# SBUF start addresses of matmul operands in a fused attention and MLP kernel: tiles moved to one byte address modulo 256

## The chip, the cores and the metric

The kernel runs on one core of one Trainium2 chip. The metric is device time in microseconds of one execution. The profile is one execution on the chip, taken by the hardware profiler. Engines are named PE (TensorE matmul), PEld (TensorE weight load), DVE (VectorE), ACT (ScalarE), POOL (GpSimd) and SP (the queue that issues most DMAs); L12 is line 12 of the kernel.

## The reference

One input x of 2048 tokens with 448 features goes through two branches, mixed by a gate per token. `_gelu` is the tanh approximation, `_layernorm` subtracts the mean and divides by the root of variance plus 1e-5.

```
def _A_ref(x, wq, wk, wv, wo):                      # 16 heads of 28, one shared key and value head
    q = (x @ wq).reshape(B, S, H, Dh).transpose(0, 2, 1, 3)
    k = x @ wk; v = x @ wv
    p = _softmax(einsum("bhqd,bkd->bhqk", q, k) * Dh ** -0.5)
    o = einsum("bhqk,bkd->bhqd", p, v)
    return o.transpose(0, 2, 1, 3).reshape(B, S, H * Dh) @ wo

def _B_ref(x, w1, w2, w3, w4):
    h = _gelu(_layernorm(x) @ w1)                   # 448 x 448
    hs = concat(four quarters of h, shifted by +1, -1, +2, -2 tokens) @ w2
    x1 = x + hs
    return x1 + _gelu(_layernorm(x1) @ w3) @ w4     # w3 448 x 1792, w4 1792 x 448

g = sigmoid((x * gate_w).sum(-1))
out = g * _A_ref(x) + (1 - g) * _B_ref(x)
```

## The kernel before

Tokens are taken in four blocks b of 512. The work goes through three stages, each with its own pool of SBUF tiles.

Stage 1 (pools s1 and s1b) projects queries, keys, values and gate (`stage_q`, with the halves wqh and wql of the weights), then does the first two MLP products (`stage_w1`, `stage_w2`). To keep precision, a matrix is split into a high part rounded to the format that TensorE multiplies in one pass, and a low part, the rest. `proj` (L134 to L140) then makes a product out of 11 matmuls: three chunks c of 128 features with high x high, low x high and high x low, and two for the last 64 features, whose high and low parts of x share one tile. In `proj`, wh and wl are the weights that are loaded into the array (LDWEIGHTS), ah and al the values that are moved through it. `stage_w1` does four column groups m of 112 columns for each block, 16 groups in all. The profile names its output h, and that of the query projection q.

Stage 2 (pool s2, and s2a on the right side of the memory) does w3 and w4. For each block b it runs a loop over f, 14 chunks of 128 hidden features. Turn f makes g, the product with w3 (`w3_part`: `proj` with ah3 and al3 moved and a column group of w3h and w3l as weights, 11 matmuls of 512 columns), takes its Gelu into gh (high) and gl (low), and then does the product of chunk f - 2 with w4 into the four accumulators acc (`w4_part`, L692 to L694: 12 matmuls of 448 columns, in which the slices of gh and gl of 128 tokens are the weights and w4h and w4l are moved). The last chunk of the last block is left to the attention stage (gf_late, w4_late). The matrices w3 and w4 lie in seven pieces of two chunks. Pieces 0 to 2 (f = 0 to 5) come from s2a, pieces 3 to 6 (f = 6 to 13) from s2, whose tiles follow those of the pool `keep` low in the memory.

Stage 3 (pool s3) is attention. There are 16 units u (block b, group g of four heads) with 16 key tiles kt of 128 keys each. A cycle handles two key tiles. `scores` (L205) does three rounds for a tile (qh with kh, ql with kh, qh with kl), each of four matmuls at once, one head in each 32 rows of the array; a slice of kh or kl of 128 keys is the weight, the queries qh and ql of 512 tokens are moved. ACT takes exponentials (L871) into p, partly after a DVE copy (L928). `values` (L882) multiplies p, moved, with vext, the values of one key tile, as weights, in single precision, and `wo_products` (L830) the result with wo. Unit 0 uses the queries qh0 and ql0, which come from another pool than qh and ql of the later units.

Instructions of all engines are written out in the order in which they run; no scheduler moves them. A pool gives a tile its byte address in each partition by the order and size of allocation, in whole steps of 32 bytes. The start addresses modulo 256 that this gives for the operands of the matmuls (a chunk or slice adds a multiple of 256, except where several are listed):

| product | moved | weights |
|---|---|---|
| q (L136 to L140) | x, 224 | wqh, wql, 224 |
| h (w1), m = 0, 1, 2, 3 | x, 224 | w1h, w1l, 224, 160, 96, 32 |
| g (w3), f = 0 to 5 | ah3, al3, 160 | w3h, w3l, 160 |
| g (w3), f = 6 to 13 | ah3, al3, 160 | w3h, w3l, 224 |
| acc (w4), f = 0 to 5 | w4h, w4l, 160 | gh, gl, 224 |
| acc (w4), f = 6 to 13 | w4h, w4l, 224 | gh, gl, 224 |
| scores, unit 0 | qh0, ql0, 32 | kh, 32; kl, 128 |
| scores, later units | qh, ql, 160 | kh, 32; kl, 128 |
| values | p, 160 | vext, 128 and 0 by turns |
| wo | wof, 224 and 96 | on, 160 and 32 by turns |
| w4 of the last chunk | w4_late, 32 and 160 | gf_late, 32 and 160 by turns |

Of the kernel before, what the change touches and what calls it, by code (L numbers as in the profile page):

```python
# [9 lines left out]
F32 = mybir.dt.float32  # L10
F32R = mybir.dt.float32r
# [6 lines left out]
P = 128  # L18
S = 2048
D = 448  # L20
# [3 lines left out]
C = D // 4  # L24
NB = S // 512
NT = S // P
# [11 lines left out]
def f32(ap):  # L38
    return ap.bitcast(F32)
# [3 lines left out]
def gated_mix_kernel(  # L43
# [14 lines left out]
    keep = ctx.enter_context(tc.tile_pool(name="keep", bufs=1))  # L58
# [8 lines left out]
    ident = keep.tile([P, P], F32, name="ident")  # L67
    make_identity(nc, ident)
    x1 = keep.tile([P, NT, D], F32, name="x1")
    kl = keep.tile([P, S], F32R, name="kl")  # L70
    vext = keep.tile([P, NT, 32], F32, name="vext")
    gz = keep.tile([P, NT], F32, name="gz")
    gg = keep.tile([P, NT], F32, name="gg")
    gi = keep.tile([P, NT], F32, name="gi")
    first = keep.tile([P, 4], F32, name="first")
    epst = keep.tile([P, 4], F32, name="epst")
    powt = keep.tile([P, 4], F32, name="powt")
    invE = keep.tile([P, NT], F32, name="invE")
    qd = dram.tile([NG, P, S], F32, name="qd")
    nc.gpsimd.memset(epst, EPS)  # L80
# [29 lines left out]
    def split_w_high(raw, wh, wl):  # L110
        nc.scalar.copy(wh[:, 0:3, :], raw[:, 0:3, :])
        nc.gpsimd.memset(f32(wh)[64:128, 3, :], 0.0)
        nc.scalar.copy(wh[0:64, 3, :], raw[0:64, 3, :])
        nc.scalar.copy(wl[64:128, 3, :], raw[64:128, 3, :])

    def split_w_low(raw, wh, wl):
        for c in range(3):
            nc.vector.tensor_tensor(wl[:, c, :], raw[:, c, :], f32(wh)[:, c, :], ALU.subtract)
        nc.vector.tensor_tensor(wl[0:64, 3, :], raw[0:64, 3, :], f32(wh)[0:64, 3, :], ALU.subtract)
# [14 lines left out]
    def proj(ps, wh, wl, ah, al):  # L134
        for c in range(3):
            nc.tensor.matmul(ps, wh[:, c, :], ah[:, c, :], start=(c == 0), stop=False)  # L136
            nc.tensor.matmul(ps, wh[:, c, :], al[:, c, :], start=False, stop=False)  # L137
            nc.tensor.matmul(ps, wl[:, c, :], ah[:, c, :], start=False, stop=False)  # L138
        nc.tensor.matmul(ps, wh[:, 3, :], ah[:, 3, :], start=False, stop=False)  # L139
        nc.tensor.matmul(ps, wl[:, 3, :], ah[:, 3, :], start=False, stop=True)  # L140
# [119 lines left out]
    with tc.tile_pool(name="s1b", bufs=1) as s1b, \  # L260
            tc.tile_pool(name="ps1", bufs=1, space=PSUM) as ps1:
        s1_stack = ExitStack()
        s1 = s1_stack.enter_context(tc.tile_pool(name="s1", bufs=1))
        turn = [0]

        def mm1(name):
            k = turn[0] % 4
            turn[0] += 1
            return mm_tile(name) if k < 2 else ps1.tile([P, 512], F32, tag="tp", bufs=2, name=name)
# [22 lines left out]
            nc.scalar.dma_start(wqraw[:, c, :], wq[:, c, :])  # L292
            nc.sync.dma_start(xraw[0][:, c, :], xT[:, c, 0:512])
        nc.scalar.activation(first, powt, AF.Gelu_apprx_tanh)
        w1h = s1.tile([P, 4, D], F32R, name="w1h")
        w1l = s1.tile([P, 4, D], F32R, name="w1l")
        w2h = s1b.tile([P, 4, D], F32R, name="w2h")
        w2l = s1b.tile([P, 4, D], F32R, name="w2l")
        hh, hl, acts = {}, {}, {}
# [31 lines left out]
        def stage_q(u, tile_of=mm1):  # L331
            b, g = divmod(u, NG)
            ps = tile_of(f"q_{u}")
            w = slice(g * P, (g + 1) * P)
            proj(ps, wqh[:, :, w], wql[:, :, w], *xact[b])
            q_out(u, ps)
# [91 lines left out]
        def spare_h(b):  # L428
            low = f32(hl[b])
            nc.sync.dma_start(shifted(hh[b], 0, 2), low[0:32, 0, 1:513])  # L430
            nc.sync.dma_start(shifted(hh[b], 2, 2), low[32:64, 0, 1:513])
            nc.sync.dma_start(shifted(hl[b], 1, 2), low[64:96, 0, 1:513])
            nc.sync.dma_start(shifted(hl[b], 3, 1), low[96:112, 0, 1:513])
# [4 lines left out]
        def stage_w1(b, between=None):  # L438
            hh[b] = s1b.tile([P, 4, 516], F32R, tag="hh", bufs=2, name=f"hh_{b}")
            hl[b] = s1b.tile([P, 4, 516], F32R, tag="hl", bufs=2, name=f"hl_{b}")  # L440
            for tt in (hh, hl):
                if b == 0:
                    nc.gpsimd.memset(f32(tt[b])[0:C, :, 0:2], 0.0)
                else:
                    nc.gpsimd.tensor_copy(tt[b][0:C, :, 0:2], f32(tt[b - 1])[0:C, :, 512:514])
            for m in range(4):
                ps = mm1(f"h_{b}_{m}")
                w = slice(m * C, (m + 1) * C)
                proj(ps[0:C, :], w1h[:, :, w], w1l[:, :, w], *xact[b])
                if between:  # L450
                    between(m)
                hf = s1.tile([P, 512], F32, tag="hf", bufs=3, name=f"hf_{b}_{m}")
                nc.vector.tensor_mul(hf[0:C, :], ps[0:C, :], rb_of[b][0:C, :])
                nc.scalar.activation(hh[b][0:C, m, 2:514], hf[0:C, :], AF.Gelu_apprx_tanh)
                nc.scalar.activation(hf[0:C, :], hf[0:C, :], AF.Gelu_apprx_tanh)
                nc.gpsimd.tensor_tensor(hl[b][0:C, m, 2:514], hf[0:C, :], f32(hh[b])[0:C, m, 2:514],
                                        ALU.subtract)
            if b in (0, 2):
                spare_h(b)
            for tt in (hh, hl):  # L460
                if b:
                    nc.gpsimd.tensor_copy(tt[b - 1][0:C, :, 514:516], f32(tt[b])[0:C, :, 2:4])
                if b == NB - 1:
                    nc.gpsimd.memset(f32(tt[b])[0:C, :, 514:516], 0.0)
# [16 lines left out]
        w1raw = f32(s1b.tile([P, 4, 516], F32R, tag="hl", bufs=2, name="w1raw"))[:, :, 0:D]  # L481
# [28 lines left out]
        centre_w1()  # L510
        stage_q(7)
        stage_q(8)
        split_w_high(w1raw, w1h, w1l)
        split_w_low(w1raw, w1h, w1l)
        for t in range(4):
            ln1_tile(1, t)
        stage_q(9)
# [9 lines left out]
        def first_between(m):  # L527
# [3 lines left out]
            if m == 2:  # L531
                ln1_send(1)
                ln1_read(1)
                spare_w2()

        stage_w1(0, first_between)

        def second(m):
# [4 lines left out]
            else:  # L543
                ln1_tile(2, 2 * m // 3)
                ln1_tile(2, 2 * m // 3 + 1)

        stage_w1(1, second)
        stage_kv(0)
        stage_kv(1)
# [11 lines left out]
        ln1_tile(3, 3)  # L561
        mv0, rs0 = stats_tiles(s1, "m")
        stage_w1(2, lambda t: stats_tile(s1, 0, t, mv0))
        stats_end(mv0, rs0)
        ln1_send(3)
# [93 lines left out]

    with tc.tile_pool(name="s2", bufs=1, reuse_waits="tile") as s2, \  # L660
            tc.tile_pool(name="ps2", bufs=1, space=PSUM, reuse_waits="tile") as ps2:
        def weigh_x1(n0, n1):
            for n in range(n0, n1):
                nc.gpsimd.tensor_scalar(x1[:, n, :], x1[:, n, :], gi[:, n:n + 1], None, op0=ALU.mult)
# [31 lines left out]
        for b in range(NB):  # L696
            acc = [ps2.tile([P, 512], F32, tag="acc", bufs=4, name=f"acc_{b}_{t}") for t in range(4)]
            gs = {}
            for f in range(NF):
# [22 lines left out]
                if b == NB - 1 and f == 4:  # L722
                    weigh_x1(0, 4 * b)
# [31 lines left out]
    with tc.tile_pool(name="s3", bufs=1, reuse_waits="tile") as s3, \  # L755
# [92 lines left out]
            if g == NG - 1 and u < NU - 1 and cols.stop == D:  # L848
                nc.sync.dma_start(out[0, n * P:(n + 1) * P, :], ot_of[n])

        pick = s3.tile([P, 4], F32, name="pick")
        nc.gpsimd.memset(pick, 0.0)
        for j in range(4):
            nc.gpsimd.memset(pick[32 * j:32 * j + 1, j:j + 1], 1.0)
# [1 line left out]
        nc.gpsimd.memset(ones, 1.0)  # L856

        weigh_x1(NT - 4, NT)

        def w4_products(t, ps, cols):  # L860
# [51 lines left out]
        for c in range(NC):  # L912
            u, i = divmod(c, NT // 2)
            k = 2 * c
            s0, s1, s2, s3_ = singles if c % 2 == 0 else singles[2:] + singles[:2]
# [19 lines left out]
            if i == 3 and norms:  # L935
                w = norms[0][0]
# [107 lines left out]
        with tc.If(again > 0, label="redo"):  # L1044
            for b in range(NB):
                for g in range(NG):
# [7 lines left out]
                    for kt in range(NT):  # L1054
                        ps = [bank(f"s2_{u}_{kt}_{j}") for j in range(4)]
                        scores(u, kt, ps)
                        p = s3.tile([P, 4, 512], F32, tag="p", bufs=PB, name=f"p2_{u}_{kt}")
# [65 lines left out]
```

## Time and profile before

| | |
|---|---|
| median of 3 runs | 924.17 us (922.94 to 924.70) |
| the profiled execution | 923.3 us |
| its span, first to last instruction | 921.4 us |
| mean granted TensorE clock | 0.999 |
| stage 1 and 2, up to the first score of unit 0 | 0 to about 401 us, of it w3 and w4 from 125 us |
| attention | about 401 us to the end |

The page of the profile first gives the busy time of each engine with its share of the span, then the chain of work that ended last. In rows of groups, the numbers behind the bar are busy time, the mean duration of one instruction in ns and the idle time just before. A matmul's duration runs on while the next one has started, so that several lie over each other; how far apart two matmuls start is read from the starts, or from a window that holds a known number of them. In rows of windows stand the stretch in us from the span's start, its length, the busy time of PE with the number of instructions that touch the window, the granted clock, the DMA share and GB/s. In rows of the timeline stand start (us), length (us), engine, line, operation and, at the end, how many equal instructions are merged into the row.

### The profile page before, as it was taken

The page shows a single profiled execution, that of the slowest core. Times are in us where ns is not written, and L with a number is a line of the kernel's source. Part 1 is how long each engine was busy: PE and PEld are TensorE (multiplying, and loading weights), DVE is VectorE, ACT ScalarE, POOL GpSimd, SP SyncE. Part 2 cuts the span into 40 slices and gives each one's busy share as a digit, 9 for nine tenths or more (in the row PEclk, how much of TensorE's full clock was granted, in tenths as well). Part 3 has the DMA queues.
Part 4 walks back from the last instruction along what each step waited for, and adds up shares of the span by engine and source line. Part 5 has one row for each costly group of instructions (what it writes and reads, how often), then busy time and mean ns, then how long its engine had stood idle before and what let it go on. Part 6 is the DMA issues. An engine that isn't in the chain of part 4 may idle for free.

```text
span 921.4 us, 24273 instructions
## 1 busy us (share of the span) xinstructions
PE 908.7 (99%) x10360; PEld 625.4 (68%) x10360; DVE 519.2 (56%) x962; ACT 635.1 (69%) x1002; POOL 79.1 (9%) x116
## 2 busy tenths in 40 slices
PE   9999999999999999999999999999999999999997
PEld 6788888888888888865555555555555555555554
DVE  4664264631431431156766767677667667676664
ACT  5442445322222232169999999999999999999994
POOL 3243420200000520020000000000000000000000
PEclk9999999999999999999999999999999999999999
DMA  8832643120110110010000001000001000010001
GB/s 305 292 88 59 172 149 109 40 66 1 41 47 1 40 46 1 1 51 24 17 22 22 16 17 53 24 25 15 25 33 37 22 20 19 15 54 14 15 14 43
DMA packets 40583, 47.32 MB, mean 51 GB/s; under 512 B 10136, under 2 KB 28632, under 8 KB 40472
## 3 DMA queue, kind: packets, MB, share of 16 engines
q1 hardware_dynamic: 37304, 40.30, 14.6%
q10 hardware_dynamic: 3168, 5.44, 1.6%
q8 instruction: 82, 1.34, 0.6%
q14 instruction: 29, 0.24, 0.1%
HBM read 32.56 MB, written 11.67 MB: 48 GB/s over the span
## 4 chain that ended last, share of the span: by engine, by line
PE 94%; ACT 4%; issue 1%; DMA 1%; DVE 0%; ACTq 0%; DVEq 0%
PE bank L882 26%; PE bank L205 17%; PE bank L830 6%; PE acc L694 5%; PE acc L692 5%; PE acc L693 5%; PE g L137 4%; PE g L138 4%; PE g L136 4%; ACT p L871 4%; PE pair L205 2%; PE hs L471 1%; PE hs L472 1%; PE g L140 1%; PE g L139 1%; PE h L136 1%
## 5 line engine op out<-in xcount | busy, mean ns | idle before, releaser
L871 ACT ACTIVATE p<-bank 128x512 f32<-128x512 f32 x512 | 265.6, 613 | 10.5 <-POOL ones L856 4.3
L882 PE MATMUL bank<-p,vext 128*32 128x256 f32 x4064 | 247.6, 382 | 6.5 <-ACT p L871 1.7
L882 PEld LDWEIGHTS bank<-p,vext 128*32 128x32 f32 x4064 | 117.6, 109 | 124.6 <-ACT p L871 61.8
L928 DVE COPY p<-pair 128x1024 f32<-128x1024 f32 x127 | 155.6, 1225 | 59.0 <-PE pair L205 46.8
L682 ACT ACTIVATE gh<-g 128x512 fp32r<-128x512 f32 x55 | 32.9, 598 | 186.4 <-PE g L140 186.4
L804 DVE TENSOR_TENSOR o<-o,bank 128x256 f32<-128x256 f32 x222 | 93.6, 422 | 85.4 <-PE bank L882 74.1
L871 ACT ACTIVATE p<-p 128x1024 f32<-128x1024 f32 x127 | 140.0, 1103 | 0.0
L871 ACT ACTIVATE p<-pair 128x1024 f32<-128x1024 f32 x129 | 137.7, 1067 | 0.0
L684 DVE TENSOR_TENSOR gl<-gf,gh 128x512 fp32r<-128x512 f32 x55 | 38.2, 694 | 169.0 <-ACT gf L683 169.0
L205 PE MATMUL bank<-qh,kh 32*128 32x512 f32 x512 | 114.8, 442 | 0.0
L205 PE MATMUL pair<-qh,kh 32*128 32x512 f32 x512 | 114.3, 441 | 0.3 <-DVE x L749 0.3
L205 PE MATMUL bank<-qh,kl 32*128 32x512 f32 x512 | 101.9, 390 | 0.0
L205 PE MATMUL pair<-qh,kl 32*128 32x512 f32 x512 | 101.6, 390 | 0.0
L205 PE MATMUL bank<-ql,kh 32*128 32x512 f32 x512 | 101.2, 388 | 0.0
L205 PE MATMUL pair<-ql,kh 32*128 32x512 f32 x512 | 100.7, 388 | 0.0
L205 PEld LDWEIGHTS bank<-qh,kh 32*128 32x128 f32 x512 | 48.2, 181 | 61.4 <-issue 37.3
L694 PE MATMUL acc<-w4h,gl 128*128 128x448 f32 x220 | 80.4, 366 | 0.0
L692 PE MATMUL acc<-w4h,gh 128*128 128x448 f32 x220 | 80.3, 365 | 0.0
L693 PE MATMUL acc<-w4l,gh 128*128 128x448 f32 x220 | 80.1, 364 | 0.0
L830 PE MATMUL bank<-wof,on 128*32 128x224 f32 (+1 forms) x984 | 69.5, 357 | 0.3 <-DVE o L804 0.2
L137 PE MATMUL g<-al,w3h 128*128 128x512 f32 x168 | 65.9, 393 | 0.0
L138 PE MATMUL g<-ah,w3l 128*128 128x512 f32 x168 | 65.9, 392 | 0.0
(206 smaller groups left out, 1394.6 us busy)
## 6 DMA issues: line engine op xcount, KB each, us to landing
qd<-qf ACTq DMA_DIRECT2D x15, 256.0 KB
rb<-rd SPq DMA_DIRECT2D x15, 256.0 KB
x<-in_x_dram SPq DMA_DIRECT2D x4, 896.0 KB
xd<-xt SPq DMA_DIRECT2D x16, 224.0 KB
w34raw<-in_w_dram SPq DMA_DIRECT2D x7, 512.0 KB
qr<-qd SPq DMA_DIRECT2D x64, 56.0 KB
w34raw<-in_w_dram SPq DMA_DIRECT2D x7, 448.0 KB
out_dram<-ot SPq DMA_DIRECT2D x14, 224.0 KB
```

The costliest lines, as they stand in the source:

```text
L136: nc.tensor.matmul(ps, wh[:, c, :], ah[:, c, :], start=(c == 0), stop=False)
L137: nc.tensor.matmul(ps, wh[:, c, :], al[:, c, :], start=False, stop=False)
L138: nc.tensor.matmul(ps, wl[:, c, :], ah[:, c, :], start=False, stop=False)
L205: nc.tensor.matmul(ps[j], k[h, keys], q[h, :], start=(r == 0), stop=(r == 2), tile_position=(32 * j, 0))
L692: nc.tensor.matmul(ps, gh[:, tok], w4h[i][:, k, :], start=(f == 0), stop=False)
L693: nc.tensor.matmul(ps, gh[:, tok], w4l[i][:, k, :], start=False, stop=False)
L694: nc.tensor.matmul(ps, gl[:, tok], w4h[i][:, k, :], start=False, stop=(f == stop))
L804: nc.vector.tensor_add(o, o, pv)
L830: nc.tensor.matmul(ps[32 * i:32 * i + 32, :], a[:, c:c + 32], w, start=start, stop=stop, tile_position=(0, 32 * i))
L871: nc.scalar.activation(p[:, heads], p[:, heads] if source is None else source, AF.Exp, scale=SCALE)
L882: nc.tensor.matmul(pv[32 * j:32 * j + 32, :], vext[:, kt, :], p_of[k][:, j, qs], start=(k == ks[0]), stop=(k == ks[-1]), tile_position=(0, ...
L928: nc.vector.tensor_copy(pa[:, both], pairs[0])
```

## The change

Tiles get other start addresses. In the pool `keep`, which lies lowest, three tiles of 16 bytes a partition and gz are allocated ahead of kl and vext, which moves kl from 128 to 32 modulo 256, and vext with it. In stage 1, w1h and w1l get 512 columns for 448: each group of 112 columns now starts at a multiple of 128 columns, so all four start at 224, and the split of w1 writes rows of 112 columns with gaps of 16 between. In stage 2 an unused tile of 192 bytes (gap2) is put ahead of the tiles of s2, which moves gh, gl, gf and pieces 3 to 6 of w3 and w4 from 224 to 160. The size of `keep` as a whole stays the same. In stage 3, pick is allocated with 36 columns and used with 4, so that the tiles behind it move on by 128 bytes: qh, ql, p, o and on go from 160 to 32. Tiles on the right side of the memory stay where they were, kh among them.

Afterwards the table reads: h 224 and 224 in all four groups; g 160 and 160 in all 14 turns; acc 160 and 160 in all turns; scores 32 for queries, kh and kl; values 32 for p, and 32 and 160 by turns for vext; wo 224 and 96 with 32 and 160; q and w4_late as before.

Every engine issues the same operations in the same order. Besides the addresses, the access patterns of the split of w1 change (three ACT copies, four DVE subtractions, a POOL memset), and some waits for DMAs that follow from which tile used an address before: ACT waits for the loads of vT at the first gf of stage 2 instead of at the first piece 3 of w3, and POOL waits for other loads of kl in the split of the keys.

```
     x1 = keep.tile([P, NT, D], F32, name="x1")
-    kl = keep.tile([P, S], F32R, name="kl")
-    vext = keep.tile([P, NT, 32], F32, name="vext")
     gz = keep.tile([P, NT], F32, name="gz")
-    gg = keep.tile([P, NT], F32, name="gg")
-    gi = keep.tile([P, NT], F32, name="gi")
     first = keep.tile([P, 4], F32, name="first")
     epst = keep.tile([P, 4], F32, name="epst")
     powt = keep.tile([P, 4], F32, name="powt")
+    kl = keep.tile([P, S], F32R, name="kl")
+    vext = keep.tile([P, NT, 32], F32, name="vext")
+    gg = keep.tile([P, NT], F32, name="gg")
+    gi = keep.tile([P, NT], F32, name="gi")
...
-        w1h = s1.tile([P, 4, D], F32R, name="w1h")
-        w1l = s1.tile([P, 4, D], F32R, name="w1l")
+        w1h = s1.tile([P, 4, 512], F32R, name="w1h")
+        w1l = s1.tile([P, 4, 512], F32R, name="w1l")
...
-                w = slice(m * C, (m + 1) * C)
+                w = slice(m * P, m * P + C)
                 proj(ps[0:C, :], w1h[:, :, w], w1l[:, :, w], *xact[b])
...
-        split_w_high(w1raw, w1h, w1l)
-        split_w_low(w1raw, w1h, w1l)
+        w1_views = [f32(w1raw).rearrange("p c (m j) -> p c m j", j=C)]
+        w1_views += [w.rearrange("p c (m j) -> p c m j", j=P)[:, :, :, 0:C] for w in (w1h, w1l)]
+        split_w_high(*w1_views)
+        split_w_low(*w1_views)
...
             tc.tile_pool(name="ps2", bufs=1, space=PSUM, reuse_waits="tile") as ps2:
+        s2.tile([P, 48], F32, name="gap2")
+
         def weigh_x1(n0, n1):
...
-        pick = s3.tile([P, 4], F32, name="pick")
+        pick = s3.tile([P, 36], F32, name="pick")[:, 0:4]
         nc.gpsimd.memset(pick, 0.0)
```

## The prediction

> **What bounds the kernel now.** I read the page first: its head, its first part and the engine shares of the chain that ended last.
>
> ```profile
> span 921.4 us, 24273 instructions
> PE 908.7 (99%) x10360; PEld 625.4 (68%) x10360; DVE 519.2 (56%) x962; ACT 635.1 (69%) x1002; POOL 79.1 (9%) x116
> PE 94%; ACT 4%; issue 1%; DMA 1%; DVE 0%; ACTq 0%; DVEq 0%
> ```
>
> TensorE works almost without a break and 94% of the chain lies on it. So what counts is how far apart matmuls start, and a change of addresses can help only there. Next I asked for busy time by window. The stage of the MLP has a natural experiment in it. In block b = 1, the windows below hold four whole turns of the f loop each, f = 2 to 5 and f = 9 to 12: 44 products with w3 (11 a turn) and 48 with w4 (12 a turn), cut at the start of a w3 group. In the first window w3 and its moved values lie at one address modulo 256 (160 and 160), in the second they do not (224 and 160). With w4 it is the other way round: 160 against 224 in the first, 224 and 224 in the second.
>
> ```profile
> 199.60:219.27 19.67, 19.67 (x93) 1.00 0.00 1
> 234.30:254.27 19.97, 19.97 (x93) 1.00 0.25 52
> ```
>
> TensorE is busy throughout both, with the same number of matmuls at a granted clock of 1.00, and the second takes 0.30 us longer. The groups of instructions in the same two windows say which matmuls it is. First window, then second:
>
> ```profile
> L694 PE MATMUL acc<-w4h,gl 128*128 128x448 f32 x16 | 5.9, 367 | 0.0
> L692 PE MATMUL acc<-w4h,gh 128*128 128x448 f32 x16 | 5.8, 363 | 0.0
> L693 PE MATMUL acc<-w4l,gh 128*128 128x448 f32 x16 | 5.8, 362 | 0.0
> L136 PE MATMUL g<-ah,w3h 128*128 128x512 f32 x12 | 4.7, 389 | 0.0
> ...
> L692 PE MATMUL acc<-w4h,gh 128*128 128x448 f32 x16 | 5.8, 365 | 0.0
> L693 PE MATMUL acc<-w4l,gh 128*128 128x448 f32 x16 | 5.8, 364 | 0.0
> L136 PE MATMUL g<-ah,w3h 128*128 128x512 f32 x12 | 4.7, 394 | 0.0
> ```
>
> The w3 product takes 389 ns with equal addresses and 394 ns with unequal ones. The w4 products show no such gain: 367, 363 and 362 with unequal addresses, 365 and 364 with equal ones.
>
> **The change part by part.** No instruction is added, removed or moved: all five engines issue the same operations in the same order. What changes are start addresses, four access patterns of the split of w1, and a few waits.
>
> *w3, the sure part.* After the change all 14 turns of each block have w3 and its moved values at 160 and 160. The eight turns f = 6 to 13 of four blocks change, 32 turns of 11 matmuls, 352 in all. The windows give 0.30 us / 44 = 6.8 ns for each, so 352 x 6.8 ns = 2.4 us. The durations would give 394 - 389 = 5 ns and 1.8 us; I take the windows, because the distance of starts makes the time and not the pipelined duration. TensorE is never idle in these windows, so it all goes to the end.
>
> *w4.* All 220 x 3 = 660 products go to 160 and 160. In the eight later turns of a block both addresses were already equal modulo 256 and both move on by the same 192 bytes; the six earlier turns become equal. By the rows above equality was worth nothing here, so I take 0. There is room on both sides. Scaled by columns from an equal group of the query projection (2.50 us for 11 below), a w4 product at the same overhead would take 2.50 / 11 x 448 / 512 = 0.199 us, while the first window leaves (19.67 - 4 x 2.50) / 48 = 0.2015 us: a gain of up to 2.5 ns each, 1.7 us in all. The other side is a state that one turn shows. These are f = 7 and f = 8 of the same block, a turn each:
>
> ```profile
> 224.27:229.27 5.00, 5.00 (x25) 1.00 0.00 0
> 229.27:234.30 5.03, 5.03 (x24) 1.00 0.00 0
> ```
>
> The second, whose w4 group (the products of f = 6) is the first with w4 and gh at equal addresses, takes 0.03 us more with the same 23 matmuls. A block has 14 w4 groups and the last has 13, 55 in all, of which four are of this kind already. If the other 51 got into that state, the cost would be 51 x 0.03 = 1.5 us.
>
> *w1.* Here only the first of four column groups was equal (224 and 224); the others stood at 160, 96 and 32 against 224. A window for each group of 11 matmuls, first a group of the query projection (equal, 128 weight columns), then the first three of w1 in block 1 (112 columns):
>
> ```profile
> 29.48:31.98 2.50, 2.50 (x13) 1.00 1.05 403
> 47.40:49.94 2.54, 2.54 (x13) 1.00 0.28 80
> 49.94:52.47 2.53, 2.53 (x12) 1.00 0.40 100
> 52.47:55.03 2.56, 2.56 (x13) 1.00 0.36 87
> ```
>
> The equal group takes 2.54, its unequal neighbours 2.53 and 2.56: with 112 columns equality buys nothing that can be seen. I take 0. The ends are the query row (16 groups x 0.04 = 0.6 us gained) and 16 x 0.01 = 0.2 us lost. The split now writes rows of 112 with gaps of 16. What it took, and when its results are first used:
>
> ```profile
> 32.40 1.32 ACT L111 CAST w1h<-w1raw 128x1344 fp32r<-128x1344 f32 x1 [0.46 <-ACT qf L316]
> 33.75 1.70 DVE L118 TENSOR_TENSOR w1l<-w1raw,w1h 128x448 fp32r<-128x448 f32 x3 [4.45 <-ACT w1h L111]
> ...
> 37.58 0.39 PE L138 MATMUL h<-ahk,w1l 128*112 128x512 f32 x1
> ```
>
> The first three parts of w1l end at 35.45 and the first of them is wanted at 37.58, so the query products cover even a doubling of the 1.70 us. If that cover were gone, TensorE would stand for what is over, well below 1 us, once. I cost it at nothing.
>
> *Waits.* ScalarE now waits at the first gf (L683) for the loads of vT, since that address was vT's before; the one row is the later of these, the other the gf:
>
> ```profile
> L348 SPq DMA_DIRECT2D vT<-qd x2: 336/376/417, 100.7 to 101.0; - x2
> ...
> 128.26 0.59 ACT L683 ACTIVATE gf<-g 128x512 f32<-128x512 f32 x1
> ```
>
> They were issued 27 us before, so nothing is held up. GpSimd's waits for loads of kl, in the split of the keys, are as far in the past. Free.
>
> *Scores and values.* Queries went from 160 to 32 and kl from 128 to 32, with kh at 32 as it was. This is a stage with two bounds. One cycle of two key tiles, on TensorE, the first instruction of each step:
>
> ```profile
> 509.40 1.93 PE L882 MATMUL bank<-p,vext 128*32 128x256 f32 x32
> 511.15 0.56 PE L830 MATMUL bank<-wof,on 128*32 128x224 f32 x8
> 511.64 0.49 PE L205 MATMUL bank<-qh,kh 32*128 32x512 f32 x2
> ...
> 512.21 0.39 PE L205 MATMUL bank<-qh,kl 32*128 32x512 f32 x2
> ...
> 512.44 0.39 PE L205 MATMUL bank<-qh,kh 32*128 32x512 f32 x2
> ...
> 513.35 0.42 PE L882 MATMUL bank<-p,vext 128*32 128x256 f32 x4
> ```
>
> and on ScalarE (line 871), this cycle's last exponential with the next cycle's first, and a place where it had no wait:
>
> ```profile
> 511.58 1.09 ACT L871 ACTIVATE p<-p 128x1024 f32<-128x1024 f32 x1
> 512.70 1.08 ACT L871 ACTIVATE p<-bank 128x512 f32<-128x512 f32 x2
> ...
> 425.41 1.09 ACT L871 ACTIVATE p<-p 128x1024 f32<-128x1024 f32 x1
> 426.36 2.10 ACT L871 ACTIVATE p<-bank 128x512 f32<-128x512 f32 x4
> ```
>
> The cycle of 3.95 us goes: values 1.75, wo 0.49, three rounds of scores of the first tile 0.80 (the second tile begins at 512.44), 0.26 until ScalarE starts at 512.70, its first exponential, and the next values at 513.35. The second tile's three rounds lie beside that exponential. ScalarE could come round 1.12 - 0.95 = 0.17 us sooner, so a gain of TensorE of up to 0.17 us a cycle would pass through. But only two distances between rounds of the first tile depend on these addresses, 0.23 us each. The distance ahead of them, 0.34 us after wo, is there in unit 0 too, where qh0 and kh are both at 32 already:
>
> ```profile
> 417.09 0.56 PE L830 MATMUL bank<-w_late,gf_late 128*32 128x224 f32 x8
> 417.58 0.50 PE L205 MATMUL bank<-qh,kh 32*128 32x512 f32 x2
> ...
> 417.92 0.39 PE L205 MATMUL bank<-ql,kh 32*128 32x512 f32 x2
> ...
> 418.15 0.40 PE L205 MATMUL bank<-qh,kl 32*128 32x512 f32 x2
> ...
> 418.38 0.41 PE L205 MATMUL bank<-qh,kh 32*128 32x512 f32 x1
> ...
> 418.64 0.40 PE L205 MATMUL bank<-ql,kh 32*128 32x512 f32 x2
> ```
>
> Unit 0 reads 0.34, 0.23, 0.23, which is the 0.80 of the cycle above, so I take 0. The best end is the query row again: 2.50 / 11 = 0.227 against 0.23, 0.003 x 2 x 128 cycles = 0.8 us gained. The worst is the last distance above, 0.26 against 0.23 in the second tile: rival E. Values and wo are single-precision products. The w4_late products of line 830 are of that kind and mix addresses of 32 and 160 on both sides; at 417.09 they take the 0.56 us, and the 0.49 until the next matmul, that the wo products with other addresses take at 511.15. So 0.
>
> **The sum.** The profiled execution took 923.3 us, 1.9 of them outside its span of 921.4. 923.3 - 2.4 = 920.9. The median of the runs, 924.17, lies 0.9 above that execution, so for a median I expect 924.2 - 2.4 = 921.8 us, 0.26% less. About 0.2%, or 1.85 us, is what a measurement of this kernel can tell from no change.
>
> **The rivals.** B: w4 follows w3, because it now enters its groups from an equal one. Gain 2.4 + 1.7 = 4.1, time 920.1. For it: w3 itself reaches 389 ns. Against it: 365 ns at 224 and 224.
>
> C: the gain of w3 is eaten, since the w4 groups fall into the state of f = 8. 2.4 - 1.5 = 0.9 gained, time 923.3. For it: that state exists and is entered at a switch to equality. Against it: in the block shown it lasted one turn: the window of f = 9 to 12 has 4.99 a turn.
>
> D: nothing changes, 924.2. The w3 tiles of the first six turns come from another pool, far up in the memory, those of the later eight from a pool low down; the 5 ns could belong to the region and not to the address modulo 256. For it: w1 and w4 gain nothing from equality. Against it: the query products, equal and in yet another place, also run at 0.227 us. The Trainium skill, TensorE: Matmul & The Clock Gate, Part 2, step 1, says that TensorE reads moved values and weights through two independent ports and that loading the next weights takes no read bandwidth from the running matmul; by it no address would matter and the sum would be 0. The rows of 389 and 394 ns, one instruction at one clock, disagree with it here.
>
> E, the other side: scores get slower. If equal addresses make a round of 32-row matmuls collide as at 418.38, 0.03 us more on the two distances of the first tile costs 2 x 128 x 0.03 = 7.7 us at most; at 0.02, as a middle, 5.1, so 924.2 - 2.4 + 5.1 = 926.9. It decides from (1.85 + 2.4) / 256 = 17 ns a round. For it: 418.38 to 418.64. Against it: in unit 0 the rounds on the path do not show it.
>
> **How the numbers follow.** My forecast has 0.48, B 0.10, C 0.20, D 0.14, E 0.08. Faster by over 0.2% are the forecast and B, less 0.01 for runs that scatter over the line: 0.57. Within it are C, D and that rest: 0.35. Slower is E: 0.08. The range goes down to B with a part of the 0.6 and 0.8 us that w1 and scores could add, 919.4, and up past D to 924.6, which leaves out E, the far end of B and a little of D, about 0.15.
>
> **What would show it.** Right: w3 products at 389 ns in all 168 of L136, and a turn of f = 9 to 12 that takes 4.92 instead of 4.99 us. w4 at 0.2015 us apart confirms the 0 there; 0.199 is B, turns that stay 0.03 us longer are C. Scores: cycles of 3.95 us as before. The forecast is wrong if late w3 products stay at 394 ns (D), or if a cycle of attention changes by more than 0.02 us either way, since 127 of them outweigh all of w3.

## The result, and the profile after

The changed kernel takes 922.54 us (median of 22 runs, 921.27 to 924.26). The kernel before, run beside it, takes 923.77 us (22 runs, 922.85 to 925.04). The ratio is 0.9984 (95% 0.9978 to 0.9991): 0.16% faster, or 1.5 us (the means lie 1.5 us apart, the medians 1.2). The interval keeps clear of 1, but the gain stays under the 0.2% (1.85 us) that the prediction had called the line. The forecast of 921.8 us was 0.7 us too low.

The page of the profile after, with the rows that answer to the first three of the prediction:

```profile
span 920.5 us, 24275 instructions
PE 907.2 (99%) x10360; PEld 626.0 (68%) x10360; DVE 519.0 (56%) x962; ACT 635.3 (69%) x1002; POOL 79.2 (9%) x116
PE 94%; ACT 4%; issue 1%; DVE 1%; DMA 1%; ACTq 0%; DVEq 0%
```

TensorE still bounds the kernel: 94% of the chain lies on it, and its busy time fell by 1.5 us. The profiled execution took 922.36 us, 1.9 of them outside its span of 920.5.

Next the two windows of four turns in block 1 once more, in the kernel after, f = 2 to 5 and f = 9 to 12:

```profile
198.95:218.70 19.75, 19.75 (x93) 1.00 0.00 1
233.52:253.28 19.76, 19.76 (x93) 1.00 0.25 50
```

Before, these were 19.67 and 19.97. The two kinds of turns have become alike, but they did not meet at the better of the two values: the late turns gained 0.21 us, or 0.05 a turn, and the early ones lost 0.08, or 0.02 a turn. (By the starts of the matmuls the early turns lost 0.06: the window of 19.67 is cut 0.01 us short.) The groups of instructions in these two windows (first window, then second; w4 has moved to L696 to L698):

```profile
L696 PE MATMUL acc<-w4h,gh 128*128 128x448 f32 x16 | 5.8, 365 | 0.0
L136 PE MATMUL g<-ah,w3h 128*128 128x512 f32 x12 | 4.7, 390 | 0.0
...
L696 PE MATMUL acc<-w4h,gh 128*128 128x448 f32 x16 | 5.8, 365 | 0.0
L136 PE MATMUL g<-ah,w3h 128*128 128x512 f32 x12 | 4.7, 390 | 0.0
```

The late w3 products went from 394 to 390 ns, and the early ones from 389 to 390. The starts at the head of a group show where that last nanosecond sits. This is the timeline of TensorE in the kernel after, from the last w4 matmul of a turn on:

```profile
233.32 0.37 PE L698 MATMUL acc<-w4h,gl 128*128 128x448 f32 x1
233.52 0.39 PE L136 MATMUL g<-ah,w3h 128*128 128x512 f32 x1
233.75 0.40 PE L137 MATMUL g<-al,w3h 128*128 128x512 f32 x1
233.99 0.39 PE L138 MATMUL g<-ah,w3l 128*128 128x512 f32 x1
234.22 0.39 PE L136 MATMUL g<-ah,w3h 128*128 128x512 f32 x1
234.44 0.39 PE L137 MATMUL g<-al,w3h 128*128 128x512 f32 x1
234.67 0.39 PE L138 MATMUL g<-ah,w3l 128*128 128x512 f32 x1
```

The first three distances are 0.23, 0.24 and 0.23 us, and only then they alternate between 0.22 and 0.23. Read to the nanosecond in the trace they are 231, 233, 231, within 1 ns in nearly all such groups, and then 227 on average to the end of the group. So an equal w3 group takes 2.508 us instead of the 2.493 that it takes at 227 ns throughout; the early turns before had 2.493. It is a cost of coming in from an equal w4 group, and after the change all w3 groups that follow a w4 group pay it.

Summed over the whole stage, by distances between starts of matmuls in the two profiled executions (us):

| part | before | after | difference |
|---|---|---|---|
| h (w1), 176 matmuls | 40.80 | 40.58 | -0.22 |
| g (w3), f = 0 to 5, 264 | 59.89 | 60.12 | +0.23 |
| g (w3), f = 6 to 13, 352 | 82.09 | 80.25 | -1.84 |
| acc (w4), 660 | 134.05 | 134.08 | +0.03 |
| first w3 matmul to first score | 276.26 | 274.68 | -1.58 |
| first score to last matmul | 515.54 | 516.34 | +0.80 |

Attention took the other half back in this execution. One window over all of it, before and then after:

```profile
401.31:916.85 515.54, 508.43 (x8515) 1.00 0.08 25
```

```profile
399.50:915.84 516.34, 509.03 (x8514) 1.00 0.08 25
```

TensorE is busy 0.6 us longer and waits 0.2 us more. Whether this comes from the new addresses is a question for the experiments. At 0.01 us no single operation of a cycle shows it. The cycle that answers to the one in the prediction, in the kernel after:

```profile
507.60 1.93 PE L886 MATMUL bank<-p,vext 128*32 128x256 f32 x32
509.35 0.56 PE L834 MATMUL bank<-wof,on 128*32 128x224 f32 x8
509.84 0.49 PE L205 MATMUL bank<-qh,kh 32*128 32x512 f32 x2
...
510.18 0.39 PE L205 MATMUL bank<-ql,kh 32*128 32x512 f32 x2
...
510.41 0.39 PE L205 MATMUL bank<-qh,kl 32*128 32x512 f32 x2
...
510.64 0.39 PE L205 MATMUL bank<-qh,kh 32*128 32x512 f32 x2
...
511.55 1.93 PE L886 MATMUL bank<-p,vext 128*32 128x256 f32 x32
```

Values 1.75, wo 0.49, rounds of scores 0.34, 0.23, 0.23, and 3.95 us to the next values: every step is as it was before, to 0.01 us. The experiment attention_undone comes back to this with the nanoseconds.

Last, the groups of w1 in the kernel after, the three of block 1 that stood at 2.54, 2.53 and 2.56:

```profile
47.37:49.89 2.52, 2.52 (x13) 1.00 0.21 75
49.89:52.40 2.51, 2.51 (x12) 1.00 0.41 131
52.40:54.92 2.52, 2.52 (x12) 1.00 0.37 88
```

They came down a little, and still lie above the 2.50 of the query projection. The first of them gained as well (2.54 to 2.52), although its weights and moved values were both at 224 before and after; what did change is the group ahead of it, which was unequal before. Block 2 went the other way: its four groups, 2.544 to 2.563 us before by the starts, take 2.563 to 2.567 after. So with 112 columns equal addresses alone do not settle the pace.

### The profile page after: what moved, and what is told of

Its sections match the earlier page's. It is cut to its first block, busy times and chain, and to the rows that moved or that the text cites. A ratio compares the mean times of both kernels' runs of the same rounds, so it can differ in the third digit from the quotient of the medians.

```text
span 920.5 us, 24275 instructions
## 1 busy us (share of the span) xinstructions
PE 907.2 (99%) x10360; PEld 626.0 (68%) x10360; DVE 519.0 (56%) x962; ACT 635.3 (69%) x1002; POOL 79.2 (9%) x116
## 4 chain that ended last, share of the span: by engine, by line
PE 94%; ACT 4%; issue 1%; DVE 1%; DMA 1%; ACTq 0%; DVEq 0%
PE bank L886 26%; PE bank L205 18%; PE bank L834 6%; PE acc L696 5%; PE acc L697 5%; PE acc L698 5%; PE g L137 4%; PE g L138 4%; PE g L136 4%; ACT p L875 4%; PE pair L205 1%; PE hs L471 1%; PE hs L472 1%; PE g L139 1%; PE g L140 1%; PE h L137 1%
## 5 line engine op out<-in xcount | busy, mean ns | idle before, releaser
L696 PE MATMUL acc<-w4h,gh 128*128 128x448 f32 x220 | 80.4, 366 | 0.0
L698 PE MATMUL acc<-w4h,gl 128*128 128x448 f32 x220 | 80.3, 365 | 0.0
```

The costliest lines, as they stand in the source:

```text
L696: nc.tensor.matmul(ps, gh[:, tok], w4h[i][:, k, :], start=(f == 0), stop=False)
L698: nc.tensor.matmul(ps, gl[:, tok], w4h[i][:, k, :], start=False, stop=(f == stop))
```

## The experiments

Three questions were open: what the w3 groups had lost, whether attention's 0.8 us came from the addresses, and which offsets between weights and moved values matter at all, and where. All kernels compute the whole reference. Diffs are against the changed kernel where nothing else is said. Times stand beside runs of the kernel before in the same session, and "blocks" is the time from the first w3 matmul to the first score.

**w4_apart.** Theory R: the w3 groups pay for coming in from an equal w4 group. Then w4 with unequal addresses gives back what the early turns had. The gap goes from the head of the pool to just ahead of piece 3: gh and gl stay at 224, while w3 and w4 lie at 160 in all turns.

```
         def load_w34(i, pool):
+            if i == 3:
+                pool.tile([P, 48], F32, name="gap2")
...
-        s2.tile([P, 48], F32, name="gap2")
```

> The changed kernel with gh, gl and gf left at 224 (the 192 bytes lie behind them), so that w3 stays equal (160 and 160) in all 14 turns while every w4 group has weights at 224 and moved values at 160. Theory R (re-entry): the slow first matmuls of each w3 group in the changed kernel (231, 233, 230 ns apart, where 227 follows) come from entering it out of an equal w4 group; then all turns take 4.92 us as the six early ones did before, the first score starts 1.0 us sooner than in the changed kernel (at about 398.5 for 399.5), and the ratio to the kernel before is about 0.9975. Rival I: a w3 group starts slowly whatever came ahead of it; turns stay at 4.94, the first score at 399.5, ratio 0.9984.

Measured: 921.81 us (11 runs) against 923.67 (21), ratio 0.9977 (0.9968 to 0.9986). The blocks took 273.65 us against 274.68 after the change and 276.26 before. The two windows of four turns, and the head of the w3 group at f = 9:

```profile
199.59:219.27 19.68, 19.68 (x93) 1.00 0.00 1
234.03:253.71 19.68, 19.68 (x93) 1.00 0.25 52
```

```profile
233.83 0.36 PE L698 MATMUL acc<-w4h,gl 128*128 128x448 f32 x1
234.03 0.39 PE L136 MATMUL g<-ah,w3h 128*128 128x512 f32 x1
234.26 0.39 PE L137 MATMUL g<-al,w3h 128*128 128x512 f32 x1
234.49 0.39 PE L138 MATMUL g<-ah,w3l 128*128 128x512 f32 x1
234.71 0.39 PE L136 MATMUL g<-ah,w3h 128*128 128x512 f32 x1
234.94 0.39 PE L137 MATMUL g<-al,w3h 128*128 128x512 f32 x1
```

Now 0.23, 0.23, 0.22, 0.23: 227 ns from the first matmul on, 2.493 us a group. The late w3 matmuls take 79.77 us in all and the early ones 59.85, 0.74 us less than after the change, and the w4 groups take 2.427 us instead of 2.432. The theory holds for the distances. In the median the gain over the changed kernel (0.0007 of the time, 0.6 us) is within what these runs can tell. (The first score came at 399.35 us and not at 398.5, since the first w3 matmul of this execution started 0.87 us later.)

**attention_undone.** Theory A: the addresses of queries, kl and vext cost attention 0.8 us. Theory N: it is the scatter from execution to execution. Both moves are taken back here, those in stages 1 and 2 stay.

```
     x1 = keep.tile([P, NT, D], F32, name="x1")
-    gz = keep.tile([P, NT], F32, name="gz")
-    first = keep.tile([P, 4], F32, name="first")
-    epst = keep.tile([P, 4], F32, name="epst")
-    powt = keep.tile([P, 4], F32, name="powt")
     kl = keep.tile([P, S], F32R, name="kl")
     vext = keep.tile([P, NT, 32], F32, name="vext")
+    gz = keep.tile([P, NT], F32, name="gz")
     gg = keep.tile([P, NT], F32, name="gg")
     gi = keep.tile([P, NT], F32, name="gi")
+    first = keep.tile([P, 4], F32, name="first")
+    epst = keep.tile([P, 4], F32, name="epst")
+    powt = keep.tile([P, 4], F32, name="powt")
...
-        pick = s3.tile([P, 36], F32, name="pick")[:, 0:4]
+        pick = s3.tile([P, 4], F32, name="pick")
```

> The changed kernel with the tiles of attention back at their old addresses (queries and p at 160, kl at 128, vext at 128 and 0); the changes to w1 and to stage 2 stay. Theory A: the 0.8 us that attention took longer in the trace of the changed kernel (516.3 for 515.5) comes from the addresses; then attention takes 515.5 again and the ratio to the kernel before falls to 0.9976. Rival N: it is scatter between executions; the ratio stays at 0.9984 within 0.0004.

Measured: 921.90 us (11 runs), ratio 0.9981 (0.9972 to 0.9990), with blocks of 274.69 us. Attention over its whole length:

```profile
399.66:916.41 516.75, 509.02 (x8515) 1.00 0.08 25
```

With the old addresses it takes 516.75 us, more than the 516.34 after the change, so the 0.8 us of theory A finds no support. The starts of the rounds show a smaller effect, though. The prediction had two distances of the first tile on the path, from ql with kh to qh with kl and from there to the second tile. Added up and averaged over 126 cycles they are 461.6 ns before, 465.4 after the change and 461.5 here.

**changed_again.** The changed kernel once more, to see how far attention of one and the same program moves.

> The changed kernel once more, on the same chip as the two above. Ratio to the kernel before 0.9984 within its interval of 0.9978 to 0.9991. Its attention in a second profiled execution: theory N (scatter) allows anything from 515.5 to 516.8 us; theory A (addresses) wants 516.3 again.

Measured: 922.09 us (11 runs) against 923.81 (15), ratio 0.9985 (0.9976 to 0.9994), so the result repeats. Blocks 274.69 us, as at first. Attention:

```profile
399.58:915.55 515.97, 509.08 (x8515) 1.00 0.08 25
```

515.97 instead of 516.34 us. Leaving out the kernel with a third set of addresses (combined_scores_64), attention took in the profiled executions 515.54, 516.75, 516.00 and 515.54 us with the old addresses (kernel before, attention_undone, stage2_alone, combined; mean 515.96), and 515.97 to 516.83 us in the eight with the new ones (mean 516.38; in one of them, multiples_of_64, kh lies 32 bytes lower). The two ranges lie over each other. The scatter sits in a few places: units 5, 6, 13 and 14 vary by 0.3 to 0.7 us from execution to execution, every other unit by less than 0.1.

The two distances of the first tile do not scatter like that. They add up to 461.5 or 461.6 ns in all four traces with the old addresses and to 464.8 to 465.6 in all eight with the new ones, 3 to 4 ns more a cycle. Over 128 cycles that is an estimate of 0.5 us against the change, if all of it reaches the end, and the means differ by 0.4. So the rounds on the path did become a little slower. That attention as a whole pays this much is not shown.

**offsets_0_96 and offsets_128_224.** Is it exact equality that w3 wants, or would a multiple of 32, 64 or 128 do? And what do other offsets do to w4? Gaps ahead of the later pieces put each at another address. In the first kernel the w3 weights of pieces 3 to 6 lie 0, 32, 64 and 96 above their moved values, in the second 128, 160, 192 and 224. The edit of the first and then of the second:

```
         def load_w34(i, pool):
+            if i > 3:
+                pool.tile([P, 8], F32, name=f"gap2_{i}")
```

```
         def load_w34(i, pool):
+            if i >= 3:
+                pool.tile([P, 32 if i == 3 else 8], F32, name=f"gap2_{i}")
```

> The changed kernel with 32 bytes more ahead of pieces 4, 5 and 6 of w3 and w4, so that the w3 weights lie 0, 32, 64 and 96 bytes (modulo 256) behind the moved values, piece by piece. Theory X (exact): only the offset 0 gives 227 ns between w3 matmuls in the settled part of a group; 32, 64 and 96 give 231 to 236. Rival Y (a smaller modulus): 32 or 96 give 227 as well. Nothing settles on w4: 2.43 us a group at every offset if equality is worth nothing there.

> The same with 128 bytes more ahead of piece 3 and 32 more ahead of each piece behind it: offsets of 128, 160, 192 and 224. Theory X: 231 to 236 ns at all four. Rival Y: 128 gives 227, so that the modulus is 128 and not 256.

Measured: one run each, 924.19 and 924.50 us, blocks 276.25 and 276.74 us, so all that the blocks had gained is gone. Windows of one w3 group of 11 matmuls in block 1, with the weights at 0, 32, 64 and 96 above the moved values (f = 7, 8, 11, 13), then, in the second kernel, at 128, 160, 192 twice and 224 (f = 6, 8, 10, 11, 13):

```profile
224.63:227.14 2.51, 2.51 (x13) 1.00 0.00 0
229.56:232.13 2.57, 2.57 (x13) 1.00 0.00 0
244.58:247.14 2.56, 2.56 (x13) 1.00 0.00 0
254.58:257.15 2.57, 2.57 (x12) 1.00 0.86 327
```

```profile
219.43:221.98 2.55, 2.55 (x12) 1.00 0.00 0
229.39:231.96 2.57, 2.57 (x12) 1.00 0.00 0
239.43:241.95 2.52, 2.52 (x12) 1.00 0.03 7
244.42:246.98 2.56, 2.56 (x12) 1.00 0.00 0
254.42:256.98 2.56, 2.56 (x12) 1.00 0.84 313
```

Only offset 0 is fast, so theory X holds in the main. Its 231 to 236 ns do not hold everywhere: at 192 the group f = 10 takes 2.52 us, 230 ns a matmul, and f = 11 takes 2.56. At 128 the group is as slow as its neighbours to within 0.02 us, so equality modulo 128 does not do. Whether w3 wants equality modulo 256 or modulo 512 stays open: by the addresses of the tiles, weights and moved values are a multiple of 512 bytes apart in every equal w3 group, and 256 was never tried. For w4, 256 is enough: an odd chunk lies 1792 bytes behind an even one, which is 256 modulo 512, and both take 2.432 us after the change. Why the offset counts at all, no run here shows.

For w4 the picture of the offsets is another one. With w4 above gh and gl by 32, 64 and 96, in windows of 12 matmuls (the products of f = 9, 10 and 13 in the first kernel):

```profile
247.14:249.60 2.46, 2.46 (x13) 1.00 0.84 162
252.17:254.58 2.41, 2.41 (x14) 1.00 0.29 36
262.02:264.48 2.46, 2.46 (x13) 1.00 0.00 0
```

Read to the nanosecond, the groups take 2.43 us at equality, 2.46 at 32 above, 2.41 at 64 above and 2.46 at 96 above; in the second kernel 2.44 to 2.45 at 128 apart, 2.46 to 2.47 at 96 below, 2.42 at 64 below and 2.45 to 2.46 at 32 below. So the 2.43 us at every offset that had been expected did not come: for w4 equality is better than 32, 96 or 128, and 64 apart is best.

**w4_64_apart.** Both are put together: w3 equal (160 and 160) in all turns, and w4 (160) 64 above gh and gl (96) in all turns.

```
         def load_w34(i, pool):
+            if i == 3:
+                pool.tile([P, 16], F32, name="gap3")
...
-        s2.tile([P, 48], F32, name="gap2")
+        s2.tile([P, 32], F32, name="gap2")
```

> The changed kernel with w3 equal at 160 and 160 and, in every w4 group, moved values (160) 64 bytes above the weights (gh and gl at 96). In the scan of offsets the w4 groups of that kind took 2.41 us for 2.43 when equal, and here every group gets it. Theory R2 (the settled distance of each product depends on its own offset, and w3 falls back to 227 at once after an unequal w4 group): turns of 4.90 us, blocks 0 to 3 together 272.7 us for 274.7 in the changed kernel, ratio to the kernel before about 0.9965. Rival: w3 starts slowly again out of these groups (14 ns each): 273.4 us.

Measured: 920.18 us (5 runs) against 923.57 (10), ratio 0.9961 (0.9948 to 0.9975). The two windows of four turns:

```profile
199.19:218.75 19.56, 19.56 (x93) 1.00 0.00 1
233.43:253.01 19.58, 19.58 (x94) 1.00 0.24 51
```

Blocks 272.21 us, 2.47 less than after the change. The w4 groups take 2.400 us, 200 ns a matmul, from the first turn to the last, better than the 2.41 of the scan, where groups before and after had other offsets. The w3 groups take 2.493 us: a w4 group at 64 apart does not cost the next group anything.

**stage2_alone.** The kernel before with the two gaps of w4_64_apart and nothing else, so without what the change does to w1 and to attention (diff against the kernel before).

```
         def load_w34(i, pool):
+            if i == 3:
+                pool.tile([P, 16], F32, name="gap3")
...
+        s2.tile([P, 32], F32, name="gap2")
```

> The kernel before with nothing changed but stage 2, where gh, gl and pieces 3 to 6 lie as in the run with w4 64 bytes apart; w1 and attention at their old addresses. Theory N: attention is worth nothing and w1 0.2 us, so the ratio is that of the run beside it, higher by 0.0002. Rival A: the new addresses of attention are worth something; the ratio differs by 0.0008 or more.

Measured: 919.63 us (6 runs), ratio 0.9966 (0.9954 to 0.9978), with blocks of 272.19 us, w1 at the old 40.80 and attention at 516.00 us. Within the intervals it is as fast as w4_64_apart: in the time of a run, the parts of the change on w1 and attention add nothing that could be measured beside it.

**multiples_of_64.** Theory L: what counts is not the offset but that start addresses are multiples of 64, so that the re-entry cost of the changed kernel comes from 160. Here all operands of stage 2 lie at 128, equal as after the change (a gap of 32 bytes in the pool `late`, ahead of s2a, and a smaller one in s2). The gap in `late` also moves kh, qh0 and ql0 from 32 to 0.

```
         w4_late = late.tile([P, D], F32, name="w4_late")
+        late.tile([P, 8], F32, name="gapl")
...
-        s2.tile([P, 48], F32, name="gap2")
+        s2.tile([P, 40], F32, name="gap2")
```

> The changed kernel with all of stage 2 moved by 32 bytes, so that w3, w4 and both their partners start at 128 modulo 256, a multiple of 64, and still at equal addresses. In the changed kernel all of them start at 160, 32 past such a multiple. Theory L: part of what is left above 512 columns at full clock is a piece of 64 bytes more that a start in mid-piece needs; the distance of w3 products falls from 227 to about 220 and the four blocks take 4 to 7 us less. Rival: only the offset between the two counts; 227 and 274.7 us as in the changed kernel.

Measured: one run, 922.50 us; blocks 274.71 us (after the change 274.68), w3 groups of 2.507 and w4 groups of 2.433 us. The theory falls: moving w3, w4 and their partners by the same 32 bytes changes nothing.

**w1_128_columns.** Why did equal addresses help w1 so little? Theory: because its weights have 112 columns. Here the gaps of 16 columns, set to zero once, are loaded with them, so that every matmul of w1 has 128 weight columns and gives 16 rows of zeros that nobody reads.

```
+        for w in (w1h, w1l):
+            nc.gpsimd.memset(f32(w).rearrange("p c (m j) -> p (c m) j", j=P)[:, :, C:P], 0.0)
...
-                w = slice(m * P, m * P + C)
-                proj(ps[0:C, :], w1h[:, :, w], w1l[:, :, w], *xact[b])
+                w = slice(m * P, (m + 1) * P)
+                proj(ps, w1h[:, :, w], w1l[:, :, w], *xact[b])
```

> The changed kernel with w1 loaded as 128 weight columns, the 16 of each gap being zeros (two more memsets on GpSimd early on), so that only the number of weight columns differs. Theory: it is the 112 columns that keep the w1 products from settling at 227 ns although their addresses are equal; with 128 a group takes 2.49 to 2.50 us for 2.53 and the 16 groups together 0.6 us less. Rival: the distance stays at 231 ns on average.

Measured: one run, 921.87 us. The three groups of w1 in block 1:

```profile
47.58:50.07 2.49, 2.49 (x12) 1.00 0.40 120
50.07:52.56 2.49, 2.49 (x12) 1.00 0.27 63
52.56:55.05 2.49, 2.49 (x12) 1.00 0.38 91
```

All 16 groups together take 40.05 us, against 40.58 after the change and 40.80 before. The row of the query projection is reached, in block 2 as well (2.493 and 2.494 us, but for its first group with 2.517): it was the 112 columns, with the 112 rows of output that go with them, that kept w1 from it.

**combined.** stage2_alone with w1_128_columns, attention as before the change.

> The kernel before with stage 2 as in the run with w4 64 bytes apart, and w1 in parts of 128 weight columns with zeros in the gaps; attention at its old addresses. Theory: the parts add up, 3.4 to 3.6 us less in stage 2 and 0.7 us less in the w1 products; ratio to the kernel before 0.9955. Rival: less w1 time only makes a later step wait; ratio 0.9966 as with stage 2 alone.

Measured: 918.27 us (5 runs, 918.24 to 918.71) against 923.81 (15), ratio 0.9941 (0.9928 to 0.9955), and 3.8 us below the 922.09 of changed_again in the same session, whose fastest run took 921.76 us. From its page, and one window each for attention and the blocks:

```profile
span 916.8 us, 24278 instructions
PE 904.5 (99%) x10360; PEld 628.6 (69%) x10360; DVE 519.0 (57%) x962; ACT 635.4 (69%) x1002; POOL 79.7 (9%) x118
```

```profile
396.81:912.35 515.54, 508.56 (x8514) 1.00 0.08 25
124.60:396.81 272.21, 272.21 (x1293) 1.00 0.16 42
```

The blocks are 4.05 us shorter than before and the w1 products 0.75, which makes 4.8 of the 5.5 us between the medians; the rest is not located. So the parts add up. Attention takes 515.54 us as before, in one execution each; the same addresses also gave 516.75.

**combined_scores_64.** Do scores like an offset of 64, as w4 does? The same as combined, but with kl at 32 as after the change (the order in `keep` is the changed one) and the queries at 96. The diff is the part that moves the queries; p and on move with them.

```
-        pick = s3.tile([P, 36], F32, name="pick")[:, 0:4]
+        pick = s3.tile([P, 52], F32, name="pick")[:, 0:4]
```

> The same with the queries at 96 and kh and kl at 32 modulo 256, so that scores too have moved values 64 bytes above the weights. If the best offset of w4 holds for scores in 32 rows, the two distances between rounds on the path fall from 0.23 to 0.227 us and attention takes up to 0.8 us less; if offsets mean nothing there, the ratio is that of the combined kernel within 0.0005, and rounds stay at 229 to 234 ns.

Measured: 919.95 us (5 runs, 919.78 to 921.63), ratio 0.9962 (0.9949 to 0.9976). Attention:

```profile
398.13:914.42 516.29, 509.54 (x8514) 1.00 0.08 25
```

516.29 us. The two distances of the first tile add up to 465.2 ns, as with the addresses of the change (464.8 to 465.6) and above the 461.5 of combined. So no gain. The runs are slower than those of combined by 1.7 us; attention holds 0.75 us of this in the profiled executions, spread over its cycles (median 3.956 us for 3.948), and another 1.3 us lies ahead of the first w3 matmul (125.92 against 124.60 us), where the edit moves nothing but kl and small tiles. That start also varies from 124.83 to 125.70 between kernels with the stage 1 of the change. How much of the 1.7 us the addresses cause stays open.

## Why the prediction was right or wrong

The main term came from where it was looked for, but smaller. That the time is only 0.7 us off is in part luck: the forecast set out from 924.2, the median of three runs, where 22 runs give 923.77, and this 0.4 us made up for part of a gain taken as 2.4 us that was 1.2 by the medians. Faster by over 0.2%, to which the prediction gave a chance of 0.57, did not come. The signs of being right, 389 ns and turns of 4.92 us, were missed by a little: 390 ns and 4.94 us.

**w3, the sure part: right in mechanism, a third of its price did not come.** Equal addresses did bring the 352 late products down, 82.09 to 80.25 us, 5.2 ns each. The failed step is the price: "the windows give 0.30 us / 44 = 6.8 ns for each". The fast window held equal w3 groups entered out of unequal w4 groups; after the change the w4 groups are equal too, and each w3 group behind one loses 0.015 us on its first three matmuls. The early turns, which the prediction left at no change, lost 0.23 us to this. So the term is -1.84 + 0.23 = -1.6 us, where 2.4 had been taken. The durations, which the prediction set aside, would have given 1.8; the price of the border is in neither. w4_apart shows the missing part directly: with w4 unequal, the same two sums come down by another 0.74 us, and 1.62 + 0.74 is the 2.4 that had been forecast.

**w4 at 0: right, with luck in the reason.** 134.05 to 134.08 us. The turns of the kernel after hold groups of 2.432 us, so neither the 0.199 us of rival B nor the slow w4 group of the turn f = 8 (2.473 us before) appeared. What the prediction could not see from its two offsets is that the best one for w4 is neither equality nor the 64 below that it had in the early turns, but 64 above. The conclusion that equality is worth nothing rested on that one other offset, 64 below (2.427 us), which happens to be a good one; at 32, 96 or 128 (2.44 to 2.47) equality would have looked worth something.

**w1 at 0, with a best end of -0.6: inside, at -0.22.** The bound from the query row is real: -0.75 us, once the weights have 128 columns. The -0.22 is the sum of gains in blocks 0, 1 and 3 and a loss of 0.06 in block 2.

**Scores, values and wo at 0: near enough, but not 0.** Rounds and cycles are as before to 0.01 us. To the nanosecond the two distances that the prediction left at nothing, because unit 0 read the same in steps of 0.01 us, got 3 to 4 ns longer a cycle together, in every trace with the new addresses. So rival E had the sign and not the size: it decided from 17 ns a round, and 2 ns came. The 0.8 us of the best end did not show.

**Rival C, the gain eaten: half right.** Its time, 923.3, is about as near to 922.54 as the forecast is, and the place, the border between equal w3 and equal w4, was the right one. Its mechanism was not: the cost was in the w3 group behind it, not in the w4 group, and it took a third of the gain, 0.8 us, where C had 1.5. C's own price was read from windows cut to 0.01 us; by the starts its w4 group lay 0.046 us above its settled neighbours (2.473 for 2.427), which makes 51 x 0.046 = 2.3 us.

**Rival D, that nothing changes: refuted.** The late pieces, low in the memory, reach 227 ns where they lie at their moved values' address. In offsets_0_96 and offsets_128_224 the region stays low and only the offset changes, and no other offset reaches 227 ns. The Trainium skill, TensorE: Matmul & The Clock Gate, Part 2, step 1, with its two independent ports, would have all of these groups alike. Here they take 2.49 or 2.51 us at equal addresses and 2.52 to 2.57 at the others.

**The sum.** Blocks -1.58 and w1 -0.22 make -1.8 us, so 923.77 - 1.8 = 922.0 us for the median beside the measured 922.54. The 0.6 us that is left lies within the scatter of attention, and the slower rounds may hold up to 0.5 of it.

## What to carry to other kernels

Where TensorE has no gap left and each matmul loads new weights, compare the distances of starts (not the durations) of equal matmuls in the same kernel whose operands lie at different offsets: a few ns each, times some hundred matmuls, is all there is to win, and here it was 0.6% with all parts together. Try the offset for each shape on its own, by shifting single tiles, since the best one was 0 for one product and 64 for its neighbour, and one offset for both products can cost something at each border between them. And price a state from rows in which the neighbours are also as they will be, for a matmul's distance depends on the group it comes from.

## What the runs showed of the hardware that was not expected

- The distance between two matmuls depends on the offset modulo 256 between the start addresses of weights and moved values: 227 ns at equality and 230 to 234 at other offsets for 512 moved columns with 128 weight columns, 200 to 206 for 448. (For the 512 columns a period of 512 is not excluded.) Groups settle into repeating patterns: 199, 207, 202, 203, 202 in an equal w4 group, and 201, 198, 201 in one 64 above.
- The pattern depends on how a group was entered: an equal w3 group starts with 231, 233, 231 behind an equal w4 group, and with 227 behind a w4 group 64 apart, above or below.
- The best offset differs by shape: 0 for the 512 moved columns of w3, and 64 above the weights for the 448 of w4 (2.400 us for 12 against 2.432 at equality and 2.46 at 32 or 96).
- 112 weight columns instead of 128 cost w1 0.53 us over 176 matmuls, 3 ns each, although a smaller matrix is loaded (174 ns a load for 188). At 112 columns, equal addresses left block 2 at 2.563 to 2.567 us a group and most others at 2.515 to 2.529.
- Shifting all operands of w3 and w4 by the same 32 bytes, from 160 to 128, changed no settled group by more than 0.001 us.
- Rounds of scores, four matmuls of 32 rows at once, got slower and not faster at equal addresses: two distances together 461.5 or 461.6 ns with the queries 128 above kh and 32 above kl, 464.8 to 465.6 with all three at one address, 465.2 with the queries 64 above both.
